# Attention over a key/value cache in decode: K and V in rows of 24 KB in place of 12 KB, wo in rows of 15 KB, and the score and value products regrouped to fit

## The chip, the cores and the metric

One Trainium2 chip, one core. The number is the device time of the program in microseconds (us). "t = 280 us" means 280 us after the first instruction of that run's profiled execution.

The engines in the profiles: PE multiplies matrices (one operand is loaded first and stays, the "stationary" one, as PEld; the other moves through), DVE and ACT work on vectors, and SP (SyncE) issues the loads. SBUF is the memory on the chip that the engines read; a DMA fills it from the chip's main memory through 16 DMA engines.

## The reference, cut to what matters

```python
# x [2,1,640]; k_cache, v_cache [2,32,8192,192]; wq [640,6144]; wo [6144,640]; all bf16
q = (layernorm(x) @ wq).reshape(2, 1, 32, 192).transpose(0, 2, 1, 3)
k = k_cache[:, :, 8192 - 2048:, :]            # the last 2048 positions
v = v_cache[:, :, 8192 - 2048:, :]
p = softmax(einsum("bhqd,bhkd->bhqk", q, k) * 192 ** -0.5)
h = x + einsum("bhqk,bhkd->bhqd", p, v).reshape(2, 1, 6144) @ wo
out = h + (gelu(layernorm(h) @ w_gate) * (layernorm(h) @ w_up)) @ w_down
```

There are 2 x 32 heads with one query each. K and V of the window are 100.7 MB, the weights 21.6 MB, and every byte is used once, so the kernel can hardly be faster than its loads.

## The kernel before

All loads go through one ring buffer in SBUF and one DMA queue. A load is issued as soon as the ring bytes under it are free, that is, when the products that read the old contents are done. A K transfer holds one head of both batches, 64 x 2 partitions with 32 positions each, so each partition is one run of 12,288 bytes in memory. The loop works in 16 groups of four (head, batch) pairs; wo comes in 16 pieces of three rows (3840 bytes) per partition. PE turns K by 768 transposes, makes the scores, and multiplies the exponentials into V.

```python
RING = 18 * 6144
def kv_src(cache, q):
    return cache[:, q, SKT - WIN:, :].rearrange("b (i t) d -> i b (t d)", t=32)
def load_k(g):
    for q in (2 * g, 2 * g + 1):
        load(("k", q), 2 * 32 * DH, kv_src(A_k_cache, q), lambda v: v)
def load_wo(g):
    load(("wo", g), 2 * 3 * D, A_wo[384 * g:384 * (g + 1), :].rearrange("(p kk) n -> p kk n", kk=3), ...)
# ... (cut)
def scores(g):                      # 24 matmuls; the moving operand steps by 4 elements
    for k in range(6):
        for j in range(4):
            r = ktr[:, (2 * g + j // 2) % KTP, k // 2, 2 * (j % 2) + k % 2:2048:4]
            e.matmul(sps[32 * j:32 * (j + 1), :], lhsT=rq[:, g % 2, j, k, :], rhs=r, ..., tile_position=(0, 32 * j))
def pv(g, h):                       # 2 x 32 matmuls of 192 columns
    for t in range(32):
        r = t % 4
        e.matmul(ops_[32 * r:32 * (r + 1), 192 * h:192 * (h + 1)], lhsT=ering[:, g % 2, h, t, :],
                 rhs=vv[:, DH * t:DH * (t + 1)], ..., tile_position=(0, 32 * r))
# ... (cut)
for g in range(NG):
    transposes(2 * g + 2); e_columns(g); o_columns(g - 1); transposes(2 * g + 3)
    oproj(g - 1); q_stationary(g + 1); pv(g, 0); scores(g + 1); pv(g, 1); softmax(g + 1)   # (guards cut)
oproj(NG - 2); o_columns(NG - 1); oproj(NG - 1)
# then layernorm, gate, up, gelu, down, and the output rows
```

## Time and profile before

| | before |
|---|---|
| time | 301.21 us, median of 3 (301.02 to 301.81) |
| span of the profiled execution | 299.5 us |
| bytes read | 122.3 MB |
| first packet, last packet of the loads | t = 2.2 us, t = 295.2 us |

The first lines are from the page of the kernel before: busy time and instruction count of each engine; the busy share of the 16 DMA engines and the rate in 40 equal slices of the span (7.5 us each, 9 is 90% or more); and the queues with packets, MB and share of 16 engines' span.

```profile
PE 237.3 (79%) x3177; PEld 191.5 (64%) x3177; DVE 131.2 (44%) x362; ACT 111.8 (37%) x138; POOL 3.2 (1%) x9
...
DMA  7999999999999999999999999999999999999992
GB/s 263 443 446 399 430 419 430 412 431 427 417 424 423 422 424 423 422 421 423 422 422 427 422 421 423 424 423 427 419 422 424 421 423 419 424 428 420 425 374 81
...
q1 hardware_dynamic: 12824, 122.30, 97.4%
q8 instruction: 24, 0.39, 0.5%
q14 instruction: 6, 0.05, 0.0%
```

The DMA row is 9 from the second slice to the last but one, while PE is busy 79%. The load queue's packets fill 97.4% of all engine time.

The next lines are from the windows view of the kernel before: the stretch, its length, busy us and instructions of each engine, PE's granted clock, the share of DMA time and GB/s.

```profile
core 0: us, PE busy (x) PEld busy (x) DVE busy (x) ACT busy (x) POOL busy (x), PEclk, DMA share, GB/s
60.00:120.00 60.00, 51.01 (x704) 41.20 (x703) 27.84 (x73) 25.57 (x31) 0.00 (x0) 0.94 1.01 424
...
180.00:240.00 60.00, 51.01 (x669) 43.57 (x671) 29.03 (x73) 24.80 (x29) 0.00 (x0) 0.91 1.01 423
```

The stream runs at 423 to 424 GB/s and its share reads 1.01.

The two lines at the head of the chain of waits of the kernel before (what the last instruction waited for, followed back; shares of the span):

```profile
DMA 58%; PE 32%; DVE 4%; ACT 2%; SPq 2%; issue 1%; DVEq 0%; ACTq 0%
DMA ring<-in_A_k_cache_dram 40%; PE tps L434 16%; DMA ring<-in_A_wq_dram 9%; DMA ring<-in_A_wo_dram 9%; PE sps L499 4%; PE m L551 3%; PE m L566 2%; SPq L264 2%; ACT eexp L512 2%; DVE mx L504 1%; PE m L549 1%; DVE ktr L446 1%; PE ops L537 1%; PE sps L616 1%; PE ops L616 1%
```

Most of the chain is DMA, and the PE pieces in it are mostly transposes that free the ring. They are on the chain because the walk passes through the ring's release; the stream never stops for them.

Two of the groups of PE work that the change rewrites (line, operation, tiles and shapes, count, then busy us and mean ns, then idle before it):

```profile
L499 PE MATMUL sps<-ktr,rq 128*32 128x512 bf16 x384 | 46.6, 632 | 0.7 <-DVE rq L321 0.5
...
L551 PE MATMUL m<-sel,osb 128*128 128x2 f32 x96 | 19.4, 318 | 0.0
```

The score matmuls take 46.6 us in total, and the fp32 products that turn output rows into columns 19.4 us.

### The profile page before, as it was taken

What the parts mean: (1) busy time and instruction counts of PE and PEld (TensorE: products, weight loads), DVE (VectorE), ACT (ScalarE), POOL (GpSimd) and SP (SyncE); (2) the same over time, 40 slices, a digit from 0 to 9 for tenths busy, and PEclk for the clock granted to TensorE, in tenths of its full rate; (3) what the DMA queues carried; (4) which work ended last, traced back from release to release, by engine and by line L of the source; (5) the groups of instructions that cost most, each with busy time, mean ns of one, the idle gap of its engine ahead of it and who ended that gap; (6) DMA issues with size and microseconds to landing.
All of it is one profiled execution on the core that took longest, in us unless ns stands there. A gap on an engine that the chain in (4) does not pass through costs nothing.

```text
span 299.5 us, 7074 instructions
## 1 busy us (share of the span) xinstructions
PE 237.3 (79%) x3177; PEld 191.5 (64%) x3177; DVE 131.2 (44%) x362; ACT 111.8 (37%) x138; POOL 3.2 (1%) x9
## 2 busy tenths in 40 slices
PE   2743689999698877959996979689597989597965
PEld 1721275868395847659583949386585958393863
DVE  5820173637254633435272627244263636172121
ACT  2320363526243634226352536232343525253000
POOL 4000000000000000000000000000000000000000
PEclk9996599799979997978999799979798999889555
DMA  7999999999999999999999999999999999999992
GB/s 263 443 446 399 430 419 430 412 431 427 417 424 423 422 424 423 422 421 423 422 422 427 422 421 423 424 423 427 419 422 424 421 423 419 424 428 420 425 374 81
DMA packets 12866, 122.74 MB, mean 410 GB/s; under 512 B 1442, under 2 KB 1444, under 8 KB 4004
## 3 DMA queue, kind: packets, MB, share of 16 engines
q1 hardware_dynamic: 12824, 122.30, 97.4%
q8 instruction: 24, 0.39, 0.5%
q14 instruction: 6, 0.05, 0.0%
q10 hardware_dynamic: 12, 0.00, 0.0%
HBM read 122.29 MB, written 0.00 MB: 408 GB/s over the span
## 4 chain that ended last, share of the span: by engine, by line
DMA 58%; PE 32%; DVE 4%; ACT 2%; SPq 2%; issue 1%; DVEq 0%; ACTq 0%
DMA ring<-in_A_k_cache_dram 40%; PE tps L434 16%; DMA ring<-in_A_wq_dram 9%; DMA ring<-in_A_wo_dram 9%; PE sps L499 4%; PE m L551 3%; PE m L566 2%; SPq L264 2%; ACT eexp L512 2%; DVE mx L504 1%; PE m L549 1%; DVE ktr L446 1%; PE ops L537 1%; PE sps L616 1%; PE ops L616 1%
## 5 line engine op out<-in xcount | busy, mean ns | idle before, releaser
L434 PE MATMUL tps<-identf,ring 128*128 128x128 f32 x768 | 108.9, 306 | 26.7 <-DMA ring<-in_A_k_cache_dram 23.2
L434 PEld LDWEIGHTS tps<-identf,ring 128*128 128x128 f32 x768 | 101.6, 162 | 30.2 <-DMA ring<-in_A_k_cache_dram 24.3
L443 ACT ACTIVATE ktr<-tps 128x1024 bf16<-128x1024 bf16 x80 | 79.4, 1023 | 70.4 <-PE tps L434 70.2
L446 DVE COPY ktr<-tps 128x1024 bf16<-128x1024 bf16 x112 | 73.7, 688 | 32.7 <-PE tps L434 30.4
L499 PE MATMUL sps<-ktr,rq 128*32 128x512 bf16 x384 | 46.6, 632 | 0.7 <-DVE rq L321 0.5
L545 ACT ACTIVATE osb<-ops 128x384 f32<-128x384 f32 x16 | 7.8, 490 | 69.8 <-PE ops L537 69.8
L504 DVE TENSOR_REDUCE mx<-sps 128x1 f32<-128x512 f32 x16 | 11.1, 692 | 49.5 <-PE sps L499 49.5
L537 PEld LDWEIGHTS ops<-ring,ering 128*32 128x32 bf16 x1024 | 23.2, 101 | 9.8 <-issue 8.8
L537 PE MATMUL ops<-ring,ering 128*32 128x192 bf16 x1024 | 28.4, 255 | 0.0
L499 PEld LDWEIGHTS sps<-ktr,rq 128*32 128x32 bf16 x384 | 11.0, 109 | 21.9 <-issue 20.9
L512 ACT ACTIVATE eexp<-sps,nm 128x1024 bf16<-128x1024 f32 x16 | 17.8, 1113 | 11.0 <-DVE nm L510 11.0
L551 PE MATMUL m<-sel,osb 128*128 128x2 f32 x96 | 19.4, 318 | 0.0
L551 PEld LDWEIGHTS m<-sel,osb 128*128 128x128 f32 x96 | 18.6, 269 | 0.0
L321 DVE TENSOR_TENSOR rq<-m,mask 128x24 bf16<-128x24 f32 x64 | 7.2, 176 | 24.2 <-PE m L478 24.2
L456 PE MATMUL tps<-ring,xnT 128*32 128x384 bf16 x80 | 5.7, 444 | 9.9 <-DMA ring<-in_A_wq_dram 9.9
L317 DVE TENSOR_SCALAR zrhs<-oh_b,zr 128x2 f32<-128x2 f32 x16 | 3.7, 229 | 20.4 <-ACT eexp L512 20.4
L566 PEld LDWEIGHTS m<-ot,ring 128*128 128x128 bf16 x240 | 11.8, 129 | 1.0 <-DVE ot L321 0.5
L508 PEld LDWEIGHTS m<-mrhs,pm 128*128 128x128 f32 x32 | 5.0, 195 | 11.5 <-DVE mrhs L317 11.5
L566 PE MATMUL m<-ot,ring 128*128 128x2 bf16 x240 | 11.6, 177 | 0.6 <-DVE ot L321 0.5
L321 DVE TENSOR_TENSOR ering<-m,bmask 128x128 bf16<-128x128 f32 x16 | 11.3, 709 | 1.5 <-PE m L522 1.0
L508 PE MATMUL m<-mrhs,pm 128*128 128x4 f32 x32 | 6.4, 269 | 7.1 <-DVE mrhs L317 7.1
L478 PE MATMUL m<-identb,qrow 2*128 2x2 bf16 x192 | 7.2, 159 | 4.6 <-DVE hT L321 3.7
(88 smaller groups left out, 88.1 us busy)
## 6 DMA issues: line engine op xcount, KB each, us to landing
ring<-in_A_k_cache_dram SPq DMA_DIRECT2D x32, 1536.0 KB, 24.5
ring<-in_A_v_cache_dram SPq DMA_DIRECT2D x32, 1536.0 KB, 28.9
ring<-in_A_wo_dram SPq DMA_DIRECT2D x16, 480.0 KB, 20.1
ring<-in_A_wq_dram SPq DMA_DIRECT2D x2, 3072.0 KB, 20.2
ring<-in_B_w_gate_dram SPq DMA_DIRECT2D x1, 1920.0 KB, 28.9
ring<-in_B_w_up_dram SPq DMA_DIRECT2D x1, 1920.0 KB, 21.1
ring<-in_A_wq_dram SPq DMA_DIRECT2D x1, 1536.0 KB, 27.4
ring<-in_B_w_down_dram SPq DMA_DIRECT2D x2, 640.0 KB, 22.8
```

The costliest lines, as they stand in the source:

```text
L321: return lambda e: e.tensor_tensor(out=out, in0=a, in1=b, op=op)
L434: ins = e.transpose(tps[bi][:, 128 * u:128 * (u + 1)], kv[:, off:off + 128], identf[:, :])
L443: act(lambda e, dst=dst, bv=bv: e.activation(out=dst, in_=bv, func=ACT.Copy), W=[("kt", slot, bank)], X=[("t", bi)])
L446: dve(lambda e, dst=dst, bv=bv: e.tensor_copy(dst, bv), W=[("kt", slot, bank)], X=[("t", bi)])
L499: ins = e.matmul(sps[32 * j:32 * (j + 1), :], lhsT=rq[:, g % 2, j, k, :], rhs=r, start=(k == 0), stop=(k == 5), tile_position=(0, 32 * j))
L504: dve(lambda e: e.tensor_reduce(out=mx[:, :], in_=sps[:, :], axis=AX.X, op=ALU.max), W=["mx"], X=["s"])
L508: pe(lambda e: e.matmul(m2[:, 0:4], lhsT=pm[:, :], rhs=mrhs[:, :], start=True, stop=True), R=["pm", "mrhs"], X=["m2"])
L512: act(lambda e: e.activation(out=eexp[:, :].rearrange("p (x d) -> p x d", d=2), in_=sps[:, :].unsqueeze(2).to_broadcast([128, 512, 2]), fu ...
L537: ins = e.matmul(ops_[32 * r:32 * (r + 1), 192 * h:192 * (h + 1)], lhsT=ering[:, g % 2, h, t, :], rhs=vv[:, DH * t:DH * (t + 1)], start=(h ...
L545: act(lambda e: e.activation(out=osb[:, :], in_=ops_[:, 0:384], func=ACT.Copy), W=["osb"], X=["o"])
L551: ins = e.matmul(m1[:, 32 + 2 * kk:34 + 2 * kk], lhsT=osb[:, kk:384:3], rhs=sel[:, :], start=True, stop=True)
L566: ins = e.matmul(m1[:, 48 + 2 * c:50 + 2 * c], lhsT=wo[:, kk, c:D:NC5], rhs=ot[:, kk, :], start=(kk == 0 and c == 0), stop=(kk == 2), skip ...
```

## The change

The intent: half as many and twice as long runs per byte of K and V, a quarter as many for wo, and fewer instructions. One transfer now holds four heads of one batch, 32 x 4 partitions with 64 positions each. Because one score matmul then sees all four heads' keys, an extra matmul adds a large negative number to the pairs of query and key that do not belong together. The ring is five slots of 24 KB. wo is loaded and multiplied in four quarters. All stationary operands for q are made before the first group.

```diff
-RING = 18 * 6144
+RING = 5 * 24576
-        def kv_src(cache, q):
-            return cache[:, q, SKT - WIN:, :].rearrange("b (i t) d -> i b (t d)", t=32)
+        def kv_src(cache, g):
+            h0 = 8 * (g // 4) + 4 * (g % 4 // 2)
+            return cache[g % 2, h0:h0 + 4, SKT - WIN:, :].rearrange("h (i t) d -> i h (t d)", t=TPG)   # TPG = 64
-            load(("wo", g), 2 * 3 * D, A_wo[384 * g:384 * (g + 1), :].rearrange("(p kk) n -> p kk n", kk=3), ...
+            load(("wo", J), 2 * 12 * D, A_wo[1536 * J:1536 * (J + 1), :].rearrange("(p kk) n -> p kk n", kk=12), ...
@@ order of the loads
-            if g != NG - 2:
-                load_wo(g)
-            if g == NG - 1:
-                load_wo(NG - 2)
+            if g % 4 == 3 and g < NG - 5:
+                load_wo(g // 4)
+        load_wo(2)
+        load_wo(3)
         load_ffn()
@@ scores
+                for ch in range(4):
+                    e.matmul(sps[32 * ch:32 * ch + 16, :], lhsT=mskl[:, :],
+                             rhs=mskr[:, :].unsqueeze(1).to_broadcast([128, 4, 128]), start=True, stop=False,
+                             tile_position=(0, 32 * ch))
                 for k in range(6):
-                    for j in range(4):
-                        r = ktr[:, (2 * g + j // 2) % KTP, k // 2, 2 * b + k % 2:2048:4]
+                    for ch in range(4):
+                        ... rhs=ktr[:, g % 2, k // 2, 1024 * ch + k % 2:1024 * (ch + 1):2] ...
@@ values
-                    ins = e.matmul(ops_[32 * r:32 * (r + 1), 192 * h:192 * (h + 1)], lhsT=ering[:, g % 2, h, t, :],
-                                   rhs=vv[:, DH * t:DH * (t + 1)], ...
+                    ins = e.matmul(ops_[32 * r:32 * r + 8, 0:384], lhsT=ering[:, g % 2, t, :],
+                                   rhs=vv[:, 384 * t:384 * (t + 1)], ...
@@ output: rows collected over four groups (fp32 selector matmuls), then columns and one projection per quarter
-            o_columns(g - 1) ... oproj(g - 1)            # 16 times, 15 matmuls each
+            o_rows(g) ... o_spread ... o_columns(J) ... oproj(J)   # 4 times, 60 matmuls each
@@ (constants, exp over 512 columns in place of 1024, and the rest cut)
```

## The prediction

> **What bounds the kernel now.** The DMA stream. The page gives queue 1 97.4% of 16 engines' span, and the windows view a DMA share of 0.99 to 1.02 at 414 to 428 GB/s in every stretch asked from 50 to 285 us. The packet records run from about 2.2 us to 295.2 us of the 299.5 us span; durations summed over 16 engines are 291.6 us, so the stream has about 1.5 us of holes. PE is busy 79%; its transposes wait for K (23 us). The last 4.3 us follow the stream.
>
> **What a packet costs (packet records, mean ns).** 3840 B (wo): 152. 12288 B (K, V): 466. 15360 B (gate, up): 579. 24576 B (wq): 916. Two 12 KB packets cost 933 against 916 for one of 24 KB: about 17 ns per packet. The Trainium skill, "DMA: Bandwidth & Descriptors", section "Why small descriptors are slow", states a fixed cost per packet; "Where 436 GB/s comes from" states a ceiling of 435 GB/s. Here 12 KB packets give 421 GB/s, 24 KB ones 429, so little is left to win.
>
> **What the change removes from the stream (critical).**
> - K and V: 8192 packets of 466.5 ns become 4096 of 916: 238.8 to 234.5 us over 16 engines, -4.3 us.
> - wo: 2048 x 152 ns becomes 512 x 579: -0.9 us.
> - 44 fewer DMAs, 16 semaphore packets of 9 ns each: -0.4 us.
> Sum -5.6 us.
>
> **What it changes off the critical path.** Scores move at a step of 2 elements instead of 4, plus 4 mask matmuls a group; PV becomes 512 x 384 columns instead of 1024 x 192; the fp32 output columns (19.4 us of PE, 96 matmuls) become 48 fp32 row matmuls; Exp reads 512 columns instead of 1024 (1.11 us each). PE busy should fall from 237 to roughly 195-215 us, ACT by about 8 us. This is worth nearly nothing while DMA bounds.
>
> **What it adds.** More constants and all 16 q stationaries before the first scores, which I expect at about 39-42 us instead of 34. The ring is coarser (5 slots of 24 KB): the tightest load (K of group 3) needs K of group 1 transposed by about 58 us, I expect 50. Later loads have over 10 us of slack. The tail: last V is followed by wo 2, wo 3 and the FFN, 23 us of stream, but two 60-matmul projections (3 us each at 50 ns), row matmuls, spreading and layernorm follow each other; my estimate is an end 0 to 1 us after what the stream alone allows: +0.4 us.
>
> **Predicted:** 301.2 - 5.6 + 0.4 = 296 us; I say 295.8, 8 in 10 within 293.4 to 298.4. Faster by over 2% (under 295.2): 0.37; within 2%: 0.60; slower: 0.03.
>
> **What would show it right.** K and V packets of 24576 B at about 916 ns; queue 1 still above 97% of the span; DMA share near 1.0 in all windows from 10 us to the end, at 426 to 430 GB/s; PE busy well down without the span following.
>
> **What would make it wrong.** Heads 3 MB apart read from four places giving slower (or faster) packets than wq's; holes in the DMA row around 40-60 us because k 1 is freed late; a tail where the two projections run cold and end over 2 us after the stream; PE lagging so that group time exceeds 14.7 us.

## More of the kernel before

The queues called "instruction" carry the program itself: 24 packets of 16 KB on q8 and a few of 8 KB on q14.

A share over 1 (the time of all packet records, divided by that of 16 engines) says that the records of consecutive packets overlap.

The end of the timeline of the kernel before (start, duration, engine, instruction; in brackets the idle time before it and what ended it):

```profile
281.90 0.73 PE L566 MATMUL m<-ot,ring 128*128 128x2 bf16 x15 [0.15 <-DMA ring<-in_A_wo_dram]
...
293.85 0.18 DVE L321 TENSOR_TENSOR uT<-ops,ga 128x24 bf16<-128x24 f32 x1 [0.68 <-PE ops L616]
...
294.09 0.83 PE L647 MATMUL m<-ring,uT 128*2 128x160 bf16 x18 [0.34 <-DVE uT L321]
295.64 1.23 PE L647 MATMUL m<-ring,uT 128*2 128x160 bf16 x30 [0.72 <-issue]
...
297.26 0.66 SPq L655 DMA_DIRECT2D out_dram<-yrow  x1
```

The last wo transfer is waited for until 281.9. From there on it is a chain of small steps: two output projections, layernorm, gate, up, gelu (`uT` at 293.85), down, output.

## The result

| | before | after |
|---|---|---|
| time, median | 301.15 us (4 runs) | 298.29 us (4 runs, 298.18 to 298.35) |
| ratio | | 0.990 (0.9883 to 0.9917) |
| span | 299.5 us | 296.4 us |
| packets of the load queue (semaphore records included) | 12,824 | 6,488 |
| mean record of a K or V packet | 466 ns (12,288 B) | 919 ns (24,576 B) |
| sum of packet records over 16 engines | 291.6 us | 286.7 us |
| last load has landed | t = 295.65 us | t = 292.23 us |
| from there to the end | 3.88 us | 4.18 us |
| PE instructions (matmul and weight load) | 6354 | 5074 |
| instruction-fetch packets of 16 KB | 24 | 19 |

A ratio is the mean time of one kernel's runs over the mean of the other's runs of the same rounds, so it is not quite the ratio of the medians quoted. The gain is 2.9 us, 1.0%, inside the predicted range and at its slow end; the point predicted was 5.4 us.

The same lines of the page of the kernel after:

```profile
PE 218.2 (74%) x2537; PEld 173.7 (59%) x2537; DVE 125.4 (42%) x295; ACT 104.9 (35%) x138; POOL 1.0 (0%) x17
...
DMA  7999999999999999999999999999999999999981
GB/s 282 436 448 420 425 425 423 437 431 433 438 403 443 428 423 430 434 430 431 425 425 426 431 425 437 427 431 427 434 423 431 427 431 423 434 416 428 427 358 43
...
q1 hardware_dynamic: 6488, 122.29, 96.7%
q8 instruction: 19, 0.31, 0.4%
q14 instruction: 3, 0.02, 0.0%
```

PE lost 19 us of busy time, DVE 6 and ACT 7, and the row of DMA digits is as full as it was. The same rows of the windows view (columns as above):

```profile
60.00:120.00 60.00, 47.11 (x511) 38.13 (x504) 22.69 (x43) 20.99 (x28) 0.00 (x0) 0.80 1.01 430
...
180.00:240.00 60.00, 50.55 (x538) 39.92 (x528) 28.64 (x53) 25.57 (x34) 0.00 (x0) 0.90 1.00 428
```

This is the gain in one view: 428 to 430 GB/s in place of 423 to 424, 1.3%. The chain of waits and the rewritten groups of the kernel after:

```profile
DMA 69%; PE 23%; ACT 3%; DVE 3%; issue 1%; SPq 1%
DMA ring<-in_A_k_cache_dram 42%; PE tps L466 12%; DMA ring<-in_A_wo_dram 10%; DMA ring<-in_A_wq_dram 9%; DMA ring<-in_A_v_cache_dram 8%; PE m L609 3%; ACT ktr L475 2%; PE ops L566 1%; ACT qrow L496 1%; DVE rq L319 1%; PE m L597 1%; PE sps L529 1%; PE sps L665 1%; PE ops L665 1%; PE m L696 1%
```

```profile
L529 PE MATMUL sps<-ktr,rq 128*16 128x512 bf16 x384 | 27.7, 426 | 0.0
...
L580 PE MATMUL m<-osb,selw 128*128 128x192 f32 x64 | 15.4, 365 | 0.0
...
L524 PE MATMUL sps<-mskr,mskl 128*16 128x512 bf16 x64 | 7.0, 425 | 3.8 <-DVE mskl L315 3.8
```

The score matmuls fell from 46.6 to 27.7 us (their step went from 4 to 2 elements and their stationary operand from 32 to 16 columns; no run separates the two), but the mask matmuls give 7.0 us back, and the row selectors take 15.4 us where the columns took 19.4. The chain holds more DMA (69% against 58%) and less PE.

The end of the timeline of the kernel after:

```profile
273.69 2.57 PE L609 MATMUL m<-ot,ring 128*128 128x2 bf16 x60 [1.77 <-DMA ring<-in_A_wo_dram]
...
290.94 0.18 DVE L319 TENSOR_TENSOR uT<-ops,ga 128x24 bf16<-128x24 f32 x1 [0.60 <-PE ops L665]
...
291.18 1.10 PE L696 MATMUL m<-ring,uT 128*2 128x160 bf16 x27 [0.28 <-DVE uT L319]
292.75 0.96 PE L696 MATMUL m<-ring,uT 128*2 128x160 bf16 x21 [0.48 <-issue]
...
294.10 0.65 SPq L704 DMA_DIRECT2D out_dram<-yrow  x1
```

The final chain now starts at the landing of wo 2, t = 273.7 us, and takes 22.7 us, where before it started at 281.9 and took 17.6.

### How the landings were read

The profiler records, for every transfer, the moment at which each of its 16 engines reports that its share has landed. The first of the 16 comes from an engine that nothing delayed; the time from one transfer's first report to the next one's is the true pace of an undelayed engine. The mean intervals in the steady part, with the number of transfers (those of wq with rows of the same length are counted in the first line):

```
                              before             after
3 MB of K or V            2 x 3.690 us (64)    7.302 us (33)
1.97 MB of wo             4 x 1.192 us (16)    4.598 us (6, with gate and up)
first 3 MB of K landed    t = 10.66 us         t = 10.35 us
```

A group's K or V costs 7.379 us as two transfers and 7.302 as one, 0.077 us less. This explains the stream: 31 x 0.077 = 2.4 us, 0.3 us for the first K, and 4 x (4.766 - 4.598) = 0.7 us for wo: 3.4 us together, and the last load did land 3.42 us earlier. My 5.6 us came from adding packet records, which overlap.

The 16 reports of the last load, in us after its first:

```
before      0.0 0.0 0.1 0.2 0.3 0.9 0.9 2.8 4.6 4.6 4.6 4.7 4.7 4.7 4.7 4.9
after       0.0 0.1 0.2 0.2 0.3 0.3 0.9 1.9 2.9 3.0 3.1 3.1 3.2 3.3 4.7 4.8
```

So the engines do not finish together. The lag grows in steps of about 1.45 us. In the kernel after, a step appears on one engine just after t = 24, 142 and 265 us, and those are the times of the 1st, 9th and 17th instruction-fetch packet. So every fetch puts one engine behind, and they go round eight engines. In both kernels the most delayed engine was hit three times, and it ends the stream. This is theory S (the number of instruction fetches sets when the stream ends). There was also a doubt: was the gain small because of the packets' true cost (theory A), or did the stream gain 5.6 us and lose half of it elsewhere (theory B)?

### The profile page after: what moved, and what is told of

The parts are those of the page before. It is cut to its first block, busy times and chain, and to the rows that moved or that the text cites. A ratio compares the mean times of both kernels' runs of the same rounds, so it can differ in the third digit from the quotient of the medians.

```text
span 296.4 us, 5662 instructions
## 1 busy us (share of the span) xinstructions
PE 218.2 (74%) x2537; PEld 173.7 (59%) x2537; DVE 125.4 (42%) x295; ACT 104.9 (35%) x138; POOL 1.0 (0%) x17
## 3 DMA queue, kind: packets, MB, share of 16 engines
q1 hardware_dynamic: 6488, 122.29, 96.7%
## 4 chain that ended last, share of the span: by engine, by line
DMA 69%; PE 23%; ACT 3%; DVE 3%; issue 1%; SPq 1%
DMA ring<-in_A_k_cache_dram 42%; PE tps L466 12%; DMA ring<-in_A_wo_dram 10%; DMA ring<-in_A_wq_dram 9%; DMA ring<-in_A_v_cache_dram 8%; PE m L609 3%; ACT ktr L475 2%; PE ops L566 1%; ACT qrow L496 1%; DVE rq L319 1%; PE m L597 1%; PE sps L529 1%; PE sps L665 1%; PE ops L665 1%; PE m L696 1%
## 5 line engine op out<-in xcount | busy, mean ns | idle before, releaser
L466 PE MATMUL tps<-identf,ring 128*128 128x128 f32 x768 | 111.0, 310 | 40.2 <-DMA ring<-in_A_k_cache_dram 39.2
L566 PE MATMUL ops<-ring,ering 128*8 128x384 bf16 x512 | 25.9, 348 | 6.9 <-DMA ring<-in_A_v_cache_dram 6.7
L543 ACT ACTIVATE eexp<-sps,nm 128x512 bf16<-128x512 f32 x16 | 11.0, 687 | 52.8 <-DVE nm L541 50.0
L529 PE MATMUL sps<-ktr,rq 128*16 128x512 bf16 x384 | 27.7, 426 | 0.0
L566 PEld LDWEIGHTS ops<-ring,ering 128*8 128x8 bf16 x512 | 11.5, 89 | 16.7 <-DMA ring<-in_A_v_cache_dram 5.7
L529 PEld LDWEIGHTS sps<-ktr,rq 128*16 128x16 bf16 x384 | 10.5, 96 | 12.7 <-issue 4.5
L580 PE MATMUL m<-osb,selw 128*128 128x192 f32 x64 | 15.4, 365 | 0.0
L580 PEld LDWEIGHTS m<-osb,selw 128*128 128x128 f32 x64 | 10.5, 197 | 7.1 <-issue 7.1
L524 PE MATMUL sps<-mskr,mskl 128*16 128x512 bf16 x64 | 7.0, 425 | 3.8 <-DVE mskl L315 3.8
L319 DVE TENSOR_TENSOR orow<-m,wm 128x1536 bf16<-128x1536 f32 (+2 forms) x5 | 8.0, 1598 | 0.2
L319 DVE TENSOR_TENSOR ering<-m,mask 128x256 bf16<-128x256 f32 x16 | 6.7, 418 | 2.0 <-PE m L551 1.9
```

The source lines that it names most:

```text
L319: return lambda e: e.tensor_tensor(out=out, in0=a, in1=b, op=op)
L466: ins = e.transpose(tps[bi][:, 128 * u:128 * (u + 1)], kv[:, off:off + 128], identf[:, :])
L529: ins = e.matmul(sps[32 * ch:32 * ch + 16, :], lhsT=rq[:, g, k, :], rhs=ktr[:, g % 2, k // 2, 1024 * ch + k % 2:1024 * (ch + 1):2], start= ...
L543: act(lambda e: e.activation(out=eexp[:, :], in_=sps[:, :], func=ACT.Exp, bias=nm[:, 0:1], scale=1.0, accum_out=zr[:, g % 2, :]), R=["nm"] ...
L566: ins = e.matmul(ops_[32 * r:32 * r + 8, 0:384], lhsT=ering[:, g % 2, t, :], rhs=vv[:, 384 * t:384 * (t + 1)], start=(t < 4), stop=(t >= 2 ...
L580: e.matmul(m1[:, 0:DH], lhsT=selw[:, tp, w:w + 128], rhs=osb[:, DH * tp:DH * (tp + 1)], start=(g % 4 == 0 and tp == 0), stop=(g % 4 == 3 a ...
```

## The experiments

All runs beside the kernel before on the same chip. The kernel after was run three more times as a control; its time hardly moves:

| run | time, median | ratio to before (95%) |
|---|---|---|
| after_same | 298.18 us | 0.9888 (0.9869 to 0.9907) |
| after_again | 298.08 us | 0.9884 (0.9866 to 0.9902) |
| after_third | 298.21 us | 0.9887 (0.9867 to 0.9907) |

> The kernel after, unchanged, as a control on this chip and beside the other runs of this call: 298.3 us, ratio to the kernel before 0.990.

> The kernel after once more, as the control of lean on the same chip: 298.2 us.

> The kernel after as the control of lean2 on the same chip: 298.1 us.

### kv12: back to rows of 12 KB, everything else as after

```diff
-P.op("sp", lambda e: e.dma_start(v, src), ...)
+for h in range(2):       # K and V only: columns 0..6143, then 6144..12287 of the same rows
+    P.op("sp", lambda e: e.dma_start(v[:, 6144 * h:6144 * (h + 1)], src[:, :, 6144 * h:6144 * (h + 1)]), ...)
```

> The kernel after, with each K or V transfer issued as two of 12 KB rows; nothing else changed. Theory A (the engines' true pace is the interval between landings: 2 x 3.691 us for 12 KB rows against 7.303 us for 24 KB rows, about 10 ns per packet removed): 32 x 0.08 = 2.5 us slower than the kernel after, less up to 0.3 us of earlier start, so 300.5 to 300.9 us. Theory B (the packet durations add up, 17 ns per packet, as I predicted, and the missing 2.5 us were lost elsewhere, in the start, the compute or the tail): 4.3 to 4.7 us slower, so 302.6 to 303.0 us.

Measured: 301.18 us (6 runs, 301.12 to 301.23), ratio 0.9984 (0.9963 to 1.0005); that is 2.9 to 3.0 us over the kernel after by the medians, 2.3 us by the spans (298.7 against 296.4), and 2.36 us by the last landing (294.58 against 292.23). The landing interval is 3.688 us, that of the kernel before, although each transfer still reads four heads of one batch: so the length of the rows sets the interval, and not which heads a transfer takes together. Two rows of the windows view:

```profile
60.00:120.00 60.00, 47.07 (x542) 38.87 (x540) 25.29 (x47) 23.24 (x31) 0.00 (x0) 0.86 1.01 425
...
180.00:240.00 60.00, 47.84 (x520) 38.18 (x508) 27.69 (x51) 24.89 (x32) 0.00 (x0) 0.91 1.01 425
```

Theory A said +2.2 to +2.6 and theory B +4.3 to +4.7. Span and landing lie in A's range; the time lies 0.3 to 0.4 us above it and over 1 us below B's. (The time is 2.6 us over the span here and 2.0 us in the kernel after. The trace has a 20th fetch packet at t = 300.43 us, after the last instruction; whether that is the reason is not shown.) With the new compute but the old rows of K and V the kernel is within noise of the one before. The new compute alone thus shows no gain; with the part of wo, next, the transfers account for all of it.

### wo4: wo back to rows of 3840 bytes

```diff
+for h in range(4):       # wo only: three of the twelve rows of each partition at a time
+    P.op("sp", lambda e: e.dma_start(v[:, 3 * h:3 * (h + 1), :], src[:, 3 * h:3 * (h + 1), :]), ...)
```

> The kernel after, with each wo transfer issued as four of 3840-byte rows. Theory A (landing intervals: 4 x 1.193 us against 4.60 us): 4 x 0.17 = 0.7 us slower, 299.0 us. Theory B (packet and semaphore durations): 1.0 us slower, 299.3 us. A rival that puts the gain in the compute alone expects no change.

Measured: 299.11 us (6 runs, 298.68 to 300.54), ratio 0.9927; 0.8 to 0.9 us over the kernel after, 0.6 us by the spans. wo's rows carry their small share; the scatter of this run is too wide to tell 0.7 from 1.0 us. Its landing intervals are 1.200 us, and four of them are 0.21 us more than one of the kernel after.

### kv6: rows of 6 KB

The edit of kv12 with four pieces of 3072 elements.

> The kernel after with each K or V transfer issued as four of 6 KB rows. Theory A (about 10 ns of engine time per packet, and 9 ns per semaphore record): three times the step of the 12 KB run, 3 x 2.5 = 7.5 us slower than the kernel after, 305.8 us; landing intervals of 6 KB transfers about 1.885 us, four of them 7.54 us against 7.303 us. Theory B (17 ns per packet): 13.5 us slower, 311.8 us.

Measured: 306.55 us (4 runs), ratio 1.0165; 8.4 us over the kernel after. The landing interval is 1.881 us, so four make 7.524 against 7.302: 24 more packets per engine in 0.222 us, 9.3 ns each with the semaphore record. From 24 to 12 KB it was 8 packets in 0.077 us, 9.6 ns. So for K and V the cost per packet is the same at both steps, near 9.5 ns, and 17 ns is refuted: theory B would have needed 13.5 us. (How it divides between the packet and the semaphore record is not shown: both steps add one record for eight packets. For wo, rows of 3,840 against 15,360 bytes, the same division gives 7.0 ns between before and after and 8.6 ns in wo4.) The span (304.65 us) rose by 8.2 us, of which the last landing accounts for 7.35; the rest is in the end of the program, where PE pauses for 1.35 us among the products of the up projection:

```profile
296.22 2.03 PE L686 MATMUL ops<-hnT,ring 128*128 128x2 bf16 x56
...
299.60 0.27 PE L686 MATMUL ops<-hnT,ring 128*128 128x2 bf16 x4 [1.35 <-issue]
```

What this pause is comes out in the next section.

### cut_instr and cut_time: does instruction fetch cost time, or does PE work?

Both give wrong attention on purpose. (The comparison with the reference, since attention is a small part of the output, proves little for this part of the kernel.)

```diff
 # cut_instr: five of six score matmuls are left out
-for k in range(6):
+for k in (5,):
 # cut_time: they stay, but move 8 columns
 for k in range(6):
+    n = 512 if k == 5 else 8
     ... sps[32 * ch:32 * ch + 16, 0:n] ... rhs=ktr[:, g % 2, k // 2, c0:c0 + 2 * n - 1:2]
```

> Wrong result on purpose: the kernel after with five of the six score matmuls per chunk left out, so 640 fewer PE instructions (320 matmuls with their weight loads), about 2.5 blocks of 16 KB of instruction fetch. Theory S (each fetch holds one DMA engine up by about 1.45 us, the fetches go round eight engines, and the engine with three of them ends the stream 4.85 us behind the first): the 17th fetch, now at 265.8 us, falls away or comes after the stream; spread of the last load's landings 3.4 us, time down by about 1.4 us to 296.9 us. Rival (PE work or the tail bounds): the same time as cut_time, whatever that is. If neither matters: 298.3 us.

> Wrong result on purpose, the control for cut_instr: the same five of six score matmuls move 8 columns instead of 512, so the number of instructions stays and about as much PE time goes. Theory S and the DMA bound: no change, 298.3 us, 19 fetches and a spread of 4.85 us. Rival (PE work bounds): as much faster as cut_instr.

Measured: cut_time 298.10 us (5 runs, ratio 0.9881), although PE's busy time fell from 218 to 207 us: the same as the kernel after, so PE work is worth nothing here. cut_instr 296.25 us (4 runs, ratio 0.9819): 1.85 us faster than its control on the same chip. It has 17 fetch packets in place of 19, and the 17th comes at t = 290.3 us in place of 265.2. (The 265.8 in the expectation was read with a wrong origin of time.) The spread of the last load's reports is 3.54 us, against 5.00 us in cut_time, and its last landing is 1.33 us earlier (290.94 against 292.26). The end of the timeline, first of cut_time, then of cut_instr:

```profile
273.40 2.56 PE L611 MATMUL m<-ot,ring 128*128 128x2 bf16 x60 [1.77 <-DMA ring<-in_A_wo_dram]
...
290.87 1.10 PE L698 MATMUL m<-ring,uT 128*2 128x160 bf16 x27 [0.28 <-DVE uT L319]
292.47 0.95 PE L698 MATMUL m<-ring,uT 128*2 128x160 bf16 x21 [0.49 <-issue]
```

```profile
272.37 2.56 PE L609 MATMUL m<-ot,ring 128*128 128x2 bf16 x60 [1.78 <-DMA ring<-in_A_wo_dram]
...
289.85 1.77 PE L696 MATMUL m<-ring,uT 128*2 128x160 bf16 x48 [0.27 <-DVE uT L319]
...
292.03 0.65 SPq L704 DMA_DIRECT2D out_dram<-yrow  x1
```

The landing that starts the final chain (wo 2) comes at 272.4 in place of 273.4 us (273.7 in the kernel after), because the most delayed engine was hit twice and not yet three times. The last 48 matmuls run in one piece of 1.77 us in place of 2.55, without the pause of 0.49 us (0.48 in the kernel after) after the 27th. The two differences, 1.0 and 0.8 us, make up the gain.

The pause is no wait for data, since the pieces of w_down end at other matmuls (16, 32, 40). The kept traces show that it stands at one place in PE's queue of instructions. Counted from the start of that queue, it comes before instruction 5057 or 5058 in the kernel after and its three controls, in cut_time, probe, kv12, wo4 and kv6 (in after_same and probe under 0.1 us of it is left). In kv6 that count falls into the up projection, and the pause is there. In the kernel before it comes before instruction 6337, which is 1280 = 5 x 256 later; and 1280 fewer PE instructions went with 5 fewer fetches, so that a block holds 256. The pause thus stands at the border of a block, and each time it ended 1.2 to 1.5 us after a fetch packet had landed. So PE waits there for its own instructions; why it goes on only so long after the landing stays open.

### probe: which engines lag

```diff
+for i, n in enumerate((8, 4, 2, 1)):      # n rows of 512 bytes behind the last load, into scratch
+    P.op("sp", lambda e, i=i, n=n: e.dma_start(probe[0:n, i, :], B_w_down[0:n, 0:256]), W=[("probe", i)], dma=f"dp{i}")
```

> The kernel after, with four small transfers of 8, 4, 2 and 1 rows issued behind the last load, to see which DMA engines lag: a transfer of 8 rows uses 8 engines, as its 8 landing records will show. If the eight engines that instruction fetch goes round are the ones these transfers use, their 8 landings spread over 0 to 4.9 us with most of them over 2.9 us behind the first landing of the last load; if they are the other eight, all land within 0.4 us, but for the one or two that lag 1 to 2 us. Time 298.3 us or up to 1 us more.

Measured, one look: 298.11 us, state unknown. The last load's 16 reports lag by 0, 0.2, 0.2, 0.3, 0.4, 0.4, 0.9, 2.0, 3.1, 3.2, 3.2, 3.5, 3.5, 3.5, 4.8 and 4.9 us. The transfer of 8 rows gave 8 reports, at 0.4, 0.4, 0.5, 0.6, 1.1, 2.1, 5.0 and 5.1 us on the same scale; that of 4 rows gave 4, at 0.6, 0.8, 1.3 and 2.3 us. So neither of my two alternatives holds: judged by their lags, the eight engines of that transfer are four that nothing delayed, the two that lag by 0.9 and 2.0 us (which fetch delayed these is not shown), and the two that were hit three times. The eight of the fetch lie across the two halves. The Trainium skill, "DMA: Bandwidth & Descriptors", section "Why a DMA increments its semaphore by 16 and not by 1", says that a transfer uses the largest number of engines, at most 16, that divides its slowest dimension, and the lowest-numbered of them; the counts of 8 and 4 reports agree, and no run here shows the numbers of the engines. To relieve the slow engines by aiming the last loads at the first eight would thus not work.

### add_instr: more instructions

```diff
+for _ in range(60):      # in every group
+    e.matmul(m2[0:8, 300:302], lhsT=identb[:, 0:8], rhs=identb[:, 0:2], start=True, stop=True)
```

> The kernel after with 60 tiny matmuls (128x8 weights, 2 columns, result never read) added per group of four heads: 1920 more PE instructions, 7.5 more blocks of 16 KB, about 3.3 us more PE time per group where PE has about 4 us to spare. Theory S: about 26 fetches; the 25th, near 276 us, is the fourth for one engine, so the spread of the last landings rises from 4.9 to about 6.3 us and the time by about 1.4 us to 299.7 us. If the spread is set by something else and PE has room: spread 4.9 us, 298.2 to 298.5 us. If PE becomes the bound, the windows would show a DMA share below 0.97 in the middle of the run, and the run decides nothing.

Measured: 298.89 us (6 runs, 298.73 to 299.12), ratio 0.991. There are 27 fetch packets, the 25th at t = 274.0 us, and the spread is 6.64 us: the step came as foretold, and the last load landed at 293.84 us, 1.6 us after that of the kernel after. PE was busy 238 us, the DMA share stayed at 1.00 to 1.01, so PE did not become the bound. The time rose by only 0.7 us, half of what I had said. The end of its timeline shows why:

```profile
293.89 0.43 PE L698 MATMUL m<-ring,uT 128*2 128x160 bf16 x8 [0.35 <-DMA ring<-in_B_w_down_dram]
...
294.73 0.66 SPq L706 DMA_DIRECT2D out_dram<-yrow  x1
```

Here the last 8 matmuls do wait for w_down, and the end comes 3.13 us after the landing. In the kernel after it comes 4.18 us after, because there the compute chain is later than the stream by 1.0 us. That slack swallowed the rest. So the stream and the chain of small steps end nearly together, and a microsecond on one of them alone is worth less than it looks.

### lean and lean2: a correct kernel with fewer instructions

cut_instr points to a version that could beat both kernels. I took out 292 PE instructions without changing what is computed, but for roundings to bf16:

```diff
-for ch in range(4): e.matmul(sps[32 * ch:32 * ch + 16, :], lhsT=mskl[:, :], ...)     # mskl [128, 16]
+e.matmul(sps[:, :], lhsT=mskl[:, :], ...)                                           # mskl [128, 128]
-osb, selw, zsel, pm, mrhs in F32, rhs=zr
+osb, selw, zsel, pm, mrhs in BF16, rhs=zrb (a bf16 copy)
 # lean only, undone in lean2:
-for r in range(4): ... m1[32 * r:32 * r + 2, 0:160] ... rhs=wd[:, f - f0, 160 * r:160 * (r + 1)]
+for r in range(2): ... m1[32 * r:32 * r + 2, 0:320] ... rhs=wd[:, f - f0, 320 * r:320 * (r + 1)]
 # ... (cut: the wider mskl, the bf16 copy zrb by DVE, and in lean the second output row tile, copied by ACT)
```

> A correct kernel: the kernel after with 292 fewer PE instructions (one mask matmul a group in place of four; the row selectors, the sums and the maxima in bf16, so two instructions less per fp32 matmul; the output rows in two tiles of 320 columns in place of four of 160). Theory S: about 1.1 blocks of instructions fewer, 18 fetches, the 17th near 280 us in place of 265.2 us, so after the landings of the last V and wo 2 that start the final chain. That chain starts 1.3 us earlier; the last load still lands near 292.2 us with a spread of 4.8 us, so about 1 us of the gain is left: 297.2 us, ratio 0.9855 to the kernel before. If the moment of the 17th fetch is nothing to the chain: 298.2 us, ratio 0.9888. The new output rows may cost or give 0.2 us of their own.

> A correct kernel: lean with the output rows of the kernel after put back (four tiles of 160), since lean's two tiles of 320 took 3.36 us for the last matmuls where the kernel after takes about 2.1. 224 fewer PE instructions than the kernel after. Theory S: the 17th fetch at about 276 us as in lean, last V and wo 2 landing 1.4 us earlier, the activations of the FFN ready at 289.8 us in place of 291.0, and the end then set by the last load's landing at 292.2 us plus 3.1 us: span 295.3 us, time 297.2 us, ratio to the kernel before 0.985 to 0.986. If the early start of the chain is worth nothing: 298.1 us.

Measured: lean 298.09 us (5 runs, control 298.08), lean2 298.13 us (4 runs, control 298.21). No gain from either. The first steps came as expected: in both the 17th fetch is at 276.3 us, and wo 2 is waited for until 272.4. In lean my own output rows took it back: the last 24 matmuls needed 3.36 us, where the 48 of four tiles take about 2.1. lean2 undid that, and its last matmuls waited for the last load:

```profile
272.39 2.56 PE L611 MATMUL m<-ot,ring 128*128 128x2 bf16 x60 [0.20 <-DMA ring<-in_A_wo_dram]
...
292.30 0.44 PE L698 MATMUL m<-ring,uT 128*2 128x160 bf16 x8 [0.34 <-DMA ring<-in_B_w_down_dram]
...
293.13 0.65 SPq L706 DMA_DIRECT2D out_dram<-yrow  x1
```

The output transfers were issued at 293.13 us, 0.9 us earlier than in the control (294.01), and yet both spans are 296.3 us. The last report of an output row came at 295.82 us in lean2 and at 295.86 in the control. The trace of lean2 shows where the 0.9 us went. Each of the two output transfers has four rows; three were reported by 294.79 and 295.01 us, the fourth at 295.63 and 295.82. The packets of these two late rows started at 294.78 and 294.80, the other six by 294.60. At 294.79 an 8 KB packet of the instruction queue q14 had ended, which started at 294.28 and took 507 ns; the control has none there. So the late rows seem to have waited behind a fetch on their DMA engine. Without it the end would have come about 0.8 us earlier (an estimate: 295.82 - 295.01), which is what theory S expected. This rests on one trace, and no run tests it. The best kernel that I can name is thus the one after.

## Why the prediction was right, and what was off

- **The bound.** Right. The stream was full before and after, and 11.6 us less PE work in cut_time moved nothing. Of the signs that I had named, the packets took 919 ns (916 said), the windows showed 426 to 430 GB/s (as said) and queue 1 filled 96.7% (over 97% said).
- **"Sum -5.6 us" for the stream.** This term was mis-sized. The runs show -3.4 us at the last landing; that the time still fell into the range is owed to its width of 5 us. The step that failed is "Two 12 KB packets cost 933 against 916 for one of 24 KB: about 17 ns per packet": records of consecutive packets overlap, and their means contain the packets that an instruction fetch held up. By landings the cost is 9.3 to 9.6 ns per packet of K and V, semaphore record included (kv12, kv6). K and V gave 2.4 us and not 4.3, the first K 0.3, and wo 0.7 and not 0.9. The trace of before already held the right number: wq's two transfers of 24 KB rows took 7.313 us each between landings, against 2 x 3.690, which would have foretold 0.07 us per 3 MB.
- **"so the stream has about 1.5 us of holes".** Wrong reading. The length of 293.0 us is that of the most delayed engine; the first engines were done 4.9 us earlier. The two errors, overlap and lag, hid each other in one sum.
- **The tail, +0.4 us.** From last landing to end it went from 3.88 to 4.18 us, +0.3, and -3.42 + 0.30 = -3.12 us is the 3.1 by which the span moved. But the three controls show 3.91, 3.91 and 4.10 us, and of the kernel before there is one trace: the term is 0 to 0.3 us, no more than the scatter of single profiles, so that 0.4 was near is in part luck.
- **Compute worth nearly nothing.** Right. PE's busy time ended at 218 us, above my 195 to 215; why is not worked out (the mask matmuls, which I had listed, took 7.0 us of it). ACT fell by 7 us.
- **The start.** Right: the first scores began at 39.2 us (I said 39 to 42), K of group 1 was turned by 49.5 (I said 50), and no hole appears near there.
- **What I had not in the sum at all:** the saved instructions. Five fetches fewer (24 to 19) were worth nothing here, because the most delayed engine had three either way (it lagged by 4.9 us before and 4.8 after). One more step down gave 1.85 us in cut_instr, through the stream and through PE's wait for instructions together.

## What to carry to other kernels

Take the cost of a transfer from the interval between landings of consecutive transfers of the same shape, on an engine that nothing delays, and not from the lengths of packet records: those overlap, and a DMA share above 1 says so. When a kernel is bound by its stream and within a few per cent of the best rate its own trace shows, look at how the stream ends: on which engine, why that one is late, and what chain of small steps runs beside it. A saved microsecond counts only up to the next of these ends. A pause that stands at the same count of instructions in several traces, and not at the same matmul, is a wait for instructions.

## What the Trainium skill lacked or had wrong

- "DMA: Bandwidth & Descriptors", section "Why small descriptors are slow", names a fixed cost per packet in cycles and in descriptor bytes; neither it nor another page gives a time per packet for rows of several KB on SyncE's queue (the one figure in ns per packet on the page is for the packets of a 4 KB transfer issued by GpSimd). Measured here: 9.3 to 9.6 ns of engine time per packet, semaphore record included, the same between 6, 12 and 24 KB rows of K and V, and 7.0 to 8.6 ns between wo's rows of 3,840 and 15,360 bytes.
- The same page, section "Where 436 GB/s comes from", gives a ceiling of 435 GB/s. This is no fault; the runs stay just below it: 3,145,728 bytes in 7.302 us is 431 GB/s with 24 KB rows and 426 GB/s with 12 KB rows (in 7.379 us).
- "Runtime: NRT & Kernel Launch", section "Instruction fetch mechanics", says that instructions come in blocks of 16 KiB by a DMA queue of the sequencer's own, and that the cost is "mostly hidden". The runs agree with the blocks (19 packets of 16,384 bytes) and not with the cost where the data stream fills all engines: each block put one of the DMA engines about 1.45 us behind, round eight of them, to a spread of 3.5, 4.8 and 6.6 us with 17, 19 and 27 blocks, and PE paused at the border of its last block (0.5 us in the kernel after, 1.35 us in kv6). Both together were worth 1.85 us of time between cut_instr and its control.
- No page says that packet records of consecutive packets overlap, so that their sum overstates the stream: 8 records of 919 ns and one of 9 make 7.36 us where transfers follow each other every 7.302.
